# One pool for exponents and front input, the last projection in other banks, the gate copied in pieces, later query loads and reordered out phases

## Chip, cores and metric

The kernel runs on one core of one Trainium2 chip. The metric is the time of one execution in microseconds of the device; lower is better. "PE" is TensorE, "DVE" VectorE, "ACT" ScalarE, "POOL" GpSimd, "SP" the engine that only issues DMAs here.

## What is computed

Two attention branches on one input x (2048 positions of 512 values, float32), mixed by a gate for each position:

```python
g = sigmoid((x * gate_w).sum(-1, keepdims=True))
# A: 32 heads of 16; each position looks at 8 positions, 2 apart, at and before it
qkv = (x @ wqkv).reshape(B, S, 3, H, Dh).transpose(2, 0, 3, 1, 4)
idx = pos[:, None] - 2 * arange(8)[None, :]           # masked where negative
a = (softmax(q . k[idx] * Dh**-0.5) @ v[idx]) @ wo
# B: 32 query heads of 16 on one shared key and value head, no mask
s = einsum("bhqd,bkd->bhqk", x @ wq (by heads), x @ wk) * Dh**-0.5
b = (softmax(s) @ (x @ wv)) @ wo
out = g * a + (1 - g) * b
```

Branch B is the heavy one: 32 heads of 2048 x 2048 scores.

## The kernel before

**Units and steps.** Branch B is cut into NU = 32 units: 512 queries (NQB = 4) times 4 heads (NHG = 8). A unit has 16 block steps, one for each 128 keys, so there are NS = 512 steps. A step multiplies keys and queries into two double banks of PSUM (`eb[0]` and `eb[1]`, named pe in the profile; `exp_pair`, L425), ACT takes the exponent of each (L427) into a tile `pexp`, and `weighted` (L435) multiplies values and exponents into the bank `po`, one step behind. The softmax's maximum is subtracted inside the score product: two extra rows of the query tile hold the maximum of each query, split in two parts. So before a unit's steps its 64 maxima over key blocks must be there. They are found by "filling": a score product into another bank (`m2`, named pm, a double bank; `m1`, named ps; in the front `po` too; L301) and a maximum on DVE, L322 for the double bank (two maxima), L333 for a single one. In the front, `fill_diff` and `fill_sum` find two key blocks' maxima at once from sums and differences of key halves (L375, L384 on ACT, L394 on DVE). `shift_a`, `shift_c` and `shift_b` bring a unit's maxima into its query tile `qst`.

**The front.** Before the blocks there are 78 "lumps" of matmuls in one list, written by `stream`: 14 lumps of queries (two more come earlier) and 64 of branch A's projections (4 groups of heads `gg` times 16 blocks of positions `j`). Lump x goes to `eb[x % 2]`. A product of full precision is made of three products of a shorter format: x is kept as a high part `xh` and a rest `xl`, and the weights likewise. A query lump's result is copied by ACT (`two`, L199), added by POOL (`qraw`), rounded by ACT (`qhi`), its rest taken by POOL (`qlo`, two buffers), and both parts go to DRAM through SP (`queries_out`, L189). Then `stack` (L274, L275) loads them, four DMAs for a unit, into one of NB = 8 tiles `qst`. A projection lump's result is copied by ACT (L238), added by DVE into `stage` (L243; the first group also into the values and the gate, L245 and L246) and stored to DRAM by a DMA on ACT's queue (L250). `half_keys` makes the sums and differences of key halves at lumps ("a", 0, 4) and ("a", 0, 6). `gates` turns the gate's 2048 values into the layout of the blocks, in 16 small copies (L263).

**The blocks.** After the last lump the front's pool is released and the pools of the second phase take its place. For each step the program writes the exponent pairs, fillings between them, and the product of the step before. The order in a step is `(0, "m2", 1, "m1")`; for the first step and after an out phase it is `(1, "m2", 0, "m1")`. POOL computes branch A beside this, group by group.

**Out phases.** Four times, `out_phase` projects 4 blocks of 128 positions with both output weights: `prepare` splits branch B's part (ACT L582, POOL L584), `turn` transposes branch A's part on PE (L591, into `eb[k]`) and splits it (ACT L597 and L598, POOL L605), the matmuls are L689, and `out_store` copies the result (`two`, ACT L624).

**Who sets the order.** The whole order is fixed when the program is built. A small planner keeps a clock for PE, ACT and DVE (`clk`), due times of banks (`free`) and of postponed work (`tasks`), with fixed costs; at every point it writes the work that its clock says is ready. Engines run their own instructions in order and wait on semaphores. What the planner does not charge, it does not see.

## Time and profile before

| what | us |
|---|---|
| median of 3 runs | 1550.73 (1546.35 to 1551.43) |
| the profiled execution, its own time | 1548.13 |
| span of that execution, first to last instruction | 1546.4 |
| PE busy | 1498.4 |
| DVE busy | 1290.7 |
| ACT busy | 1220.0 |
| POOL busy | 934.7 |

The mean granted TensorE clock was 0.992. In the profile's rows "L427" is a line of the kernel; a row of a timeline has the start, the time taken, engine, line, operation, what is written and read, and in brackets the idle time of the engine before it and what ended that; "PEld" is the load of weights, which runs beside matmuls. A row of the waits has the sum in us, the number of waits and the longest. Matmuls overlap in the rows, so the start of one to the start of the next tells its cost.

### The profile page before, as it was taken

To read this page: it belongs to the slowest core of one execution; us is meant where nothing else is said; L and a number is where in the kernel's file an instruction comes from. 1 tells how busy PE (TensorE), PEld (TensorE's weight loads), DVE (VectorE), ACT (ScalarE), POOL (GpSimd) and SP (SyncE) were. 2 spreads that over 40 slices of the span, in tenths; PEclk is the share of its full clock that TensorE was granted. 3 is DMA by queue.
4 is the path that set the end of the run, shared out by engine and by line. 5 is a ranking of instruction groups with operands and counts; after the bars stand their busy time and mean duration, and the time that the engine had idled before them with its cause. 6 is when DMAs were issued, how large, how long until landed. Compare 5 with 4: busy or idle time off the path is not lost.

```text
span 1546.4 us, 29008 instructions
## 1 busy us (share of the span) xinstructions
PE 1498.4 (97%) x11020; PEld 720.5 (47%) x11020; DVE 1290.7 (83%) x1937; ACT 1220.0 (79%) x1490; POOL 934.7 (60%) x1525
## 2 busy tenths in 40 slices
PE   7899999899999999999999999999999999999997
PEld 4788999533333333333333453333345335433532
DVE  6887888789888989989898898998889889887811
ACT  4447776589999989999899749989875985799686
POOL 7731898698898888888889888884022003100310
PEclk9999999899999999999999999999999999999999
DMA  6643243221121122112112112110000000000000
GB/s 213 186 115 120 88 149 92 70 75 47 40 74 57 39 75 74 47 40 74 40 39 72 57 41 72 40 40 11 12 18 23 11 2 15 15 1 1 1 1 28
DMA packets 44019, 85.63 MB, mean 55 GB/s; under 512 B 9616, under 2 KB 26072, under 8 KB 39784
## 3 DMA queue, kind: packets, MB, share of 16 engines
q0 software_dynamic: 6816, 37.97, 7.4%
q1 hardware_dynamic: 19160, 31.40, 6.8%
q10 hardware_dynamic: 17904, 14.42, 2.9%
q8 instruction: 86, 1.41, 0.4%
q14 instruction: 53, 0.43, 0.1%
HBM read 57.97 MB, written 25.25 MB: 54 GB/s over the span
## 4 chain that ended last, share of the span: by engine, by line
PE 87%; ACT 5%; DVE 5%; DMA 1%; POOL 1%; issue 1%; SPq 1%; DVEq 0%; ACTq 0%; POOLq 0%
PE po L435 30%; PE pe L425 21%; PE pm L301 9%; PE pe L894 9%; PE ps L301 8%; PE pe L689 5%; ACT pexp L427 4%; DVE mx L322 2%; PE pm L375 2%; PE ps L375 1%; PE pe L172 1%; PE po L375 1%; DVE mx L333 1%; DMA xraw<-xt 0%; DMA qd<-qlo 0%
## 5 line engine op out<-in xcount | busy, mean ns | idle before, releaser
L427 ACT ACTIVATE pexp<-pe 128x1024 f32<-128x1024 f32 x1022 | 988.8, 1022 | 106.7 <-PE pe L425 100.2
L322 DVE TENSOR_REDUCE mx<-pm 128x2 f32<-128x1024 f32 x565 | 688.2, 1218 | 131.3 <-PE pm L301 126.7
L435 PE MATMUL po<-pexp,vst 128*32 128x512 f32 x4088 | 545.3, 605 | 0.5 <-ACT pexp L427 0.4
L425 PE MATMUL pe<-qst,kst 64*128 64x512 f32 x2048 | 467.1, 453 | 16.4 <-ACT pexp L427 7.6
L425 PEld LDWEIGHTS pe<-qst,kst 64*128 64x128 f32 x2048 | 191.8, 184 | 523.8 <-ACT pexp L427 503.4
L333 DVE TENSOR_REDUCE mx<-ps 128x1 f32<-128x512 f32 x556 | 377.6, 679 | 7.3 <-PE ps L301 6.6
L301 PE MATMUL pm<-kst,qst 62*128 62x512 f32 x1140 | 241.1, 410 | 3.2 <-DVE mx L322 1.9
L301 PE MATMUL ps<-kst,qst 62*128 62x512 f32 x556 | 227.5, 409 | 0.7 <-DVE mx L333 0.7
L495 POOL TENSOR_TENSOR pr<-aext 128x256 f32<-128x256 f32 x256 | 182.1, 737 | 4.7 <-PE pe L894 4.5
L548 POOL TENSOR_TENSOR oa<-oa,av 128x256 f32<-128x256 f32 x224 | 163.9, 732 | 17.3
L435 PEld LDWEIGHTS po<-pexp,vst 128*32 128x32 f32 x4088 | 80.4, 108 | 175.6 <-issue 162.3
L461 POOL TENSOR_TENSOR rl<-rl,gate_t 128x16 f32<-128x16 f32 x31 | 6.8, 219 | 249.7 <-DVE rl L455 249.7
L545 POOL TENSOR_TENSOR av<-aext,lg 128x256 f32<-128x256 f32 x224 | 139.3, 622 | 13.5
L301 PEld LDWEIGHTS pm<-kst,qst 62*128 62x128 f32 x1140 | 111.4, 187 | 28.1 <-DVE mx L322 23.0
L894 PE MATMUL pe<-wah,xh 64*128 64x384 f32 (+1 forms) x512 | 117.7, 349 | 4.8 <-DVE gate L246 3.3
L894 PE MATMUL pe<-wah,xl 64*128 64x384 f32 (+1 forms) x512 | 118.2, 342 | 0.0
L894 PE MATMUL pe<-wal,xh 64*128 64x384 f32 (+1 forms) x512 | 118.0, 342 | 0.0
L384 ACT ACTIVATE dd<-pm 128x512 f32<-128x512 f32 x162 | 88.5, 596 | 35.7 <-PE pm L375 31.8
L301 PEld LDWEIGHTS ps<-kst,qst 62*128 62x128 f32 x556 | 104.1, 187 | 26.6 <-DVE mx L333 21.1
L501 POOL TENSOR_TENSOR tr<-pr 128x512 f32<-128x512 f32 x64 | 81.6, 1276 | 4.9
L501 POOL TENSOR_TENSOR tr<-tr 128x256 f32<-128x256 f32 (+1 forms) x128 | 72.3, 565 | 9.2
L894 PEld LDWEIGHTS pe<-wah,xh 64*128 64x128 f32 x512 | 72.6, 190 | 10.8 <-issue 5.6
(157 smaller groups left out, 1523.3 us busy)
## 6 DMA issues: line engine op xcount, KB each, us to landing
aext<-ad POOLq DMA_DIRECT2D x32, 1056.0 KB, 5.5
ad<-stage ACTq DMA_DIRECT2D x32, 384.0 KB
qst<-qd SPq DMA_DIRECT2D x64, 128.0 KB
xraw<-xt SPq DMA_DIRECT2D x16, 256.0 KB
qd<-qhi SPq DMA_DIRECT2D x16, 256.0 KB
qd<-qlo SPq DMA_DIRECT2D x16, 256.0 KB
qst<-qd SPq DMA_DIRECT2D x64, 64.0 KB
qst<-ml SPq DMA_DIRECT2D x220, 2.0 KB
```

Source lines behind the costliest of these rows:

```text
L301: nc.tensor.matmul(dst, qst[v % NB][b:b + 62, pr, t * P:(t + 1) * P], kst[b:b + 62, kc * 512:(kc + 1) * 512], start=True, stop=True)
L322: nc.vector.tensor_reduce(m[:, :, pr, t, kc], dst, AX.X, ALU.max)
L333: nc.vector.tensor_reduce(m[:, odd, pr, t, kc:kc + 1], dst, AX.X, ALU.max)
L384: nc.scalar.activation(dd[0][:, odd], m2[:, odd, :], AF.Abs)
L425: nc.tensor.matmul(bank[:, odd, :], kst[b:b + 64, kt * P:(kt + 1) * P], qst[u % NB][b:b + 64, pr, :], start=True, stop=True)
L427: nc.scalar.activation(e, bank, AF.Exp, scale=SCALE)
L435: nc.tensor.matmul(po[32 * i:32 * i + 32, :], vst[:, kt, :], pexp[s, i // 2][:, i % 2, :], start=(kt == 0), stop=(kt == NJ - 1))
L495: nc.gpsimd.tensor_mul(pr[:, k], q, e[:, o:o + NH, AC:2 * AC])
L501: nc.gpsimd.tensor_add(nx, cur[:, :, 0:n], cur[:, :, n:2 * n])
L545: nc.gpsimd.tensor_mul(av, e[:, o:o + NH, 2 * AC:].rearrange("p j (h d) -> p j h d", d=DH), lg[:, w].unsqueeze(3).to_broadcast([P, NH, AG, ...
L548: nc.gpsimd.tensor_add(ao, ao, av)
L894: nc.tensor.matmul(eb[x % 2][:, b, :n], l[h], r[h], start=(i == 0), stop=(i == 3 * C - 1))
```

## The change

Seven edits.

1. A pool `px` with six tiles lives through the whole kernel. The first three quarters of `xh` are six tiles of it, the last quarter is in the front's pool, and all exponents (`pexp`, and the last output tiles) take the same six tiles in turn. The tile `early` for the first step is gone.
2. The last lump writes to `m2` instead of `eb[1]`. Its list entry settles the posts of the two lumps before it and issues both exponent pairs of step 0, after its third and its eighth group of matmuls. From the last group but one of the lump before it, `ended` stops the fillings into `m2`; the sums and differences stay selected until the list's end (`formed.clear()` moves there), so no new single filling is written either.
3. After the list, the posts and the store are settled; the wait of 0.7 us on the planner's clock and two fillings are gone.
4. `gates` puts its 16 copies into `tasks`, 3 us apart, and charges 0.24 us for each.
5. `half_keys` writes only the matmuls; copies and sums come as a task 1 us later, both copies first, and the banks count as taken for 4 us.
6. `stack` is no longer called for units 4 to 7 after query lumps 2 and 3, but for one unit after each of the lumps 5, 7, 9 and 11.
7. An out phase's first `prepare` is written one step before the phase, its first `turn` after two groups of matmuls of the phase, and the rest of that split after seven. The step keeps its usual order of banks.

```diff
+    px = ctx.enter_context(tc.tile_pool(name="exps", bufs=6))
-    xh = [p1.tile([P, C, 512], F32R, name="xh", tag=f"xh{t}", bufs=1) for t in range(NQB)]
+    xh = [[px.tile([P, 2, 512], F32R, name="xh", tag="pexp", bufs=6) for k in range(2)] for t in range(3)]
+    xh.append([p1.tile([P, 2, 512], F32R, name=f"xh3{k}") for k in range(2)])
...
-            for u in (2 * m, 2 * m + 1):
-                if u < NB:
-                    stack(u)
+            if m > 4 and m % 2 and len(stacked) < NB:
+                stack(len(stacked))
...
-        for i in range(HG):
-            for b in range(4):
-                nc.scalar.activation(gate_t[32 * i:32 * i + 32, :, :, b], gate[32 * b:32 * b + 32, 1, :].rearrange("p (q j) -> p q j", j=4), AF.Copy)
+        for k in range(16):
+            tasks.append((clk["pe"] + 3.0 * (k + 1), gates_of, (32 * (k // 4), k % 4)))
+
+    def gates_of(i, b):
+        nc.scalar.activation(gate_t[i:i + 32, :, :, b], gate[32 * b:32 * b + 32, 1, :].rearrange("p (q j) -> p q j", j=4), AF.Copy)
+        after("act", 0, 0.24)
...
         clk["pe"] += 1.2
+        for k in keys:
+            free[k] = clk["pe"] + 4.0
+        tasks.append((clk["pe"] + 1.0, half_parts, (g, keys)))
+
+    def half_parts(g, keys):
         for x in range(2):
-            parts, src = kcd[0][:, g, x], hb[g][x]
-            nc.scalar.activation(parts, src, AF.Identity, scale=mk[:, 0:1])
-            at = after("act", clk["pe"] + T_LAT, 0.6)
-            nc.vector.scalar_tensor_tensor(parts, src, mk[:, 1:2], parts.bitcast(F32), op0=ALU.mult, op1=ALU.add)
+            nc.scalar.activation(kcd[0][:, g, x], hb[g][x], AF.Identity, scale=mk[:, 0:1])
+            at = after("act", clk["pe"], 0.65)
+        for x in range(2):
+            parts = kcd[0][:, g, x]
+            nc.vector.scalar_tensor_tensor(parts, hb[g][x], mk[:, 1:2], parts.bitcast(F32), op0=ALU.mult, op1=ALU.add)
...
-        e = e or pe[0].tile([P, 2, 512], F32, name="pexp", bufs=6)
+        e = px.tile([P, 2, 512], F32, name="pexp", bufs=6)
...
-            if paired():
+            if ended:
+                pass
+            elif paired():
...
     def out_phase(js, n):
-        prepare(js[0], n)
-        turn(js[0], 1)
-        later.pop(js[0])()
...
+            if x == 0 and i == 1:
+                turn(j, 1)
+            if x == 0 and i == 6:
+                later.pop(j)()
...
-        nc.tensor.matmul(eb[x % 2][:, b, :n], l[h], r[h], start=(i == 0), stop=(i == 3 * C - 1))
+        nc.tensor.matmul(front[2 if x == last else x % 2][0][:, b, :n], l[h], r[h], start=(i == 0), stop=(i == 3 * C - 1))
...
-        if x == last and i == 4:
-            early.append(p1.tile([P, 2, 2, 512], F32, name="early", tag="xh0", bufs=1))
-            exp_pair(0, 0, early[0][:, 0])
+        if x == last - 1 and i == 3 * C - 2:
+            ended.add(1)
+        if x == last and i in (2, 7):
+            settle(f"post{(i - 1) % 2}", 0)
+            exp_pair(0, int(i == 2))
...
+    front = [(eb[0], "e0"), (eb[1], "e1"), (m2, "m2")]
...
-    clk["pe"] += 0.7
-    settle("post0", 0)
-    settle("post1", 0)
-    fill_ready("m2", 0.5)
-    fill_ready("m1", 0.5)
-    exp_pair(0, 1, early[0][:, 1])
+    formed.clear()
+    for kind in ("post0", "post1", "store"):
+        settle(kind, 0)
...
-            out_phase(list(range(outs, outs + 4)), n)
-            outs += 4
-            order = (1, "m2", 0, "m1")
+            if not due:
+                prepare(outs, n)
+                due.append(n)
+            else:
+                out_phase(list(range(outs, outs + 4)), due.pop())
+                outs += 4
```

The rest of the diff follows from these: `xh[t][:, c, :]` becomes `xh[t][c // 2][:, c % 2, :]`, and due times are looked up by the bank's key.

More of the change, by code (lines that the diff above doesn't have):

```diff
@@ L115, in split_x @@
         for c in range(C):
-            split(xh[t][:, c, :], xl[:, t, c, :], xraw[t, c], eng)
+            split(xh[t][c // 2][:, c % 2, :], xl[:, t, c, :], xraw[t, c], eng)
     def load_wa(gg, c):
@@ L183, in queries @@
         cs = slice(cc * P, (cc + 1) * P)
-        return three(lambda c: wqh[:, c, cs], lambda c: wql[:, c, cs], lambda c: xh[qb][:, c, :], lambda c: xl[:, qb, c, :])
+        return three(lambda c: wqh[:, c, cs], lambda c: wql[:, c, cs], lambda c: xh[qb][c // 2][:, c % 2, :], lambda c: xl[:, qb, c, :])
     def queries_out(m, hi, lo):
@@ L222, in a_project @@
         t, r = j // 4, slice(j % 4 * P, (j % 4 + 1) * P)
-        return three(lambda c: xh[t][:, c, r], lambda c: xl[:, t, c, r], lambda c: wah[gg][:, c, :n], lambda c: wal[gg][:, c, :n])
+        return three(lambda c: xh[t][c // 2][:, c % 2, r], lambda c: xl[:, t, c, r], lambda c: wah[gg][:, c, :n], lambda c: wal[gg][:, c, :n])
     def a_post(gg, j, x):
-        bank, n = eb[x], GN + (0 if gg else VN)
+        (bank, key), n = front[x], GN + (0 if gg else VN)
         settle("post0", 0)
@@ L239, in a_post @@
         at = after("act", clk["pe"] + T_LAT, 0.45) + 0.1
-        free[f"e{x}"] = at + 1.5
+        free[key] = at + 1.5
         def rest():
@@ L246, in rest @@
                 nc.vector.tensor_add(gate[:, 1, j:j + 1], bank[:, 0, GN + DH:GN + DH + 1], two[:, GN + DH:GN + DH + 1])
-            free[f"e{x}"] = after("dve", at, 0.5 if gg else 0.75) + 0.1
+            free[key] = after("dve", at, 0.5 if gg else 0.75) + 0.1
             if j % 2 == 1:
                 dst = ad[gg * GC:(gg + 1) * GC, HALO:, :].rearrange("g (p j) n -> p g (j n)", j=NJ)
-                tasks.append((free[f"e{x}"], lambda: nc.scalar.dma_start(dst[:, :, (j - 1) * AN:(j + 1) * AN], st.rearrange("p g j n -> p g (j n)")), (), "store"))
+                tasks.append((free[key], lambda: nc.scalar.dma_start(dst[:, :, (j - 1) * AN:(j + 1) * AN], st.rearrange("p g j n -> p g (j n)")), (), "store"))
             if j == NJ - 1:
-                tasks.append((free[f"e{x}"] + 0.5, whole, (gg,)))
-        tasks.append((at, rest, (), f"post{x}"))
+                tasks.append((free[key] + 0.5, whole, (gg,)))
+        tasks.append((at, rest, (), f"post{x % 2}"))
     def gates():
@@ L335, in fill_one @@
         filled(v, 1)
-    sel, kcd, dd, pend, ready_d, formed = [], [], [], [], [0.0, 0.0], set()
+    sel, kcd, dd, pend, ready_d, formed, ended = [], [], [], [], [0.0, 0.0], set(), set()
     hb = [(m2[:, 0, :], m2[:, 1, :]), (m1, po)]
@@ L415, in shift_b, with exp_pair @@
         shifted.add(v)
-    pe, pexp, exped, early = [], {}, {}, []
-    def exp_pair(s, pr, e=None):
+    pe, pexp, exped = [], {}, {}
+    def exp_pair(s, pr):
         bank, key = eb[pr], f"e{pr}"
@@ L642, in stream @@
         at, told = [0, 0], 0
+        ended.clear()
         while min(at) < len(seq):
@@ L886, in mm @@
                 half_keys(1 if lump[2] == 4 else 0)
-            elif x == last:
-                formed.clear()
             items[x] = queries(lump[1]) if lump[0] == "q" else a_project(*lump[1:])
-            clk["pe"] = max(clk["pe"], free[f"e{x % 2}"])
+            clk["pe"] = max(clk["pe"], free["m2" if x == last else f"e{x % 2}"])
         n = 512 if lump[0] == "q" else GN + (0 if lump[1] else VN)
@@ L916, in done_mm @@
             gg, j = lump[1:]
-            a_post(gg, j, x % 2)
+            a_post(gg, j, 2 if x == last else x % 2)
             if gg + 1 < C:
@@ L942, in gated_mix_kernel @@
     pe.append(tc.alloc_tile_pool(name="weighted", bufs=1, side="right"))
-    outs = 0
+    outs, due = 0, []
     for s in range(NS + 1):
@@ L960, in gated_mix_kernel @@
         k, n = outs // 4, C - (outs >= NJ - 4)
-        if outs < NJ and outs // NH in done and (NHG * (k + 1) - 1 in shaped if n == C else s >= 16 * (NU - 2) + 4) and (lead < LEAD or s >= 16 * (NHG * (k + 2) + 1) - 3):
-            out_phase(list(range(outs, outs + 4)), n)
-            outs += 4
-            order = (1, "m2", 0, "m1")
+        if due or outs < NJ and outs // NH in done and (NHG * (k + 1) - 1 in shaped if n == C else s >= 16 * (NU - 2) + 4) and (lead < LEAD or s >= 16 * (NHG * (k + 2) + 1) - 3):
+            if not due:
[4 more added lines that the diff above has]
+                outs += 4
         elif short > 0 and steps < 2:
@@ L1010, in gated_mix_kernel @@
             j = NJ - 4 + 2 * x + t
-            os = pe[0].tile([P, D], F32, name="osl", tag="pexp", bufs=6)
+            os = px.tile([P, D], F32, name="osl", tag="pexp", bufs=6)
             nc.vector.tensor_add(os, eb[x][:, t, :], parts[j])
```

## Prediction

> **What bounds the kernel now.** I read the page first, for shares, then PE's own waits, then the clock stretch by stretch, and then the order of events around each long wait.

> ```profile
> PE 1498.4 (97%) x11020; PEld 720.5 (47%) x11020; DVE 1290.7 (83%) x1937; ACT 1220.0 (79%) x1490; POOL 934.7 (60%) x1525
> ```

> PE is the bound: busy 1498.4 of 1546.4 us. An edit that leaves the matmuls alone can win only in the other 48 us, and in stretches where busy matmuls ran at half clock. PE's waits say where the 48 us are:

> ```profile
> PE pe L425 <- ACT pexp L427: 7.6, 20, 2.1
> PE pe L425 <- ACT two L624: 5.0, 4, 1.5
> ...
> PE pe L894 <- ACT two L199: 4.1, 1, 4.1
> PE pe L894 <- DVE gate L246: 3.3, 3, 1.7
> PE pe L425 <- DVE stage L243: 2.6, 2, 1.7
> PE pm L375 <- ACT dd L384: 2.4, 1, 2.4
> PE pe L425 <- ACT early L427: 1.1, 1, 1.1
> PE pe L591 <- ACT pexp L427: 1.7, 4, 0.5
> ...
> PE pe L689 <- POOL own L584: 1.2, 1, 1.2
> ```

> Each row but the first is a place that the diff touches: L199 the query lumps, L246 the half keys, L384 the gate, L243 and "early" the hand-over from front to blocks, L624, L591 and L584 the out phases. The clock (PEclk) by windows:

> ```profile
> 60.00:63.70 3.70, 0.00 (x0) 0.00 (x0) 1.65 (x3) 1.25 (x2) 3.62 (x4) 1.00 0.70 204
> 63.70:67.10 3.40, 3.05 (x14) 2.49 (x16) 0.51 (x1) 1.37 (x3) 3.06 (x4) 0.50 0.60 154
> ...
> 149.00:155.90 6.90, 5.72 (x34) 5.52 (x36) 3.65 (x10) 4.15 (x9) 3.48 (x6) 0.51 0.95 360
> ...
> 282.20:285.60 3.40, 1.70 (x16) 1.36 (x16) 3.37 (x6) 0.35 (x1) 3.24 (x13) 1.00 0.37 116
> 285.60:289.00 3.40, 3.40 (x22) 3.10 (x18) 3.07 (x4) 1.03 (x2) 3.17 (x5) 0.50 0.02 5
> 289.00:292.40 3.40, 1.39 (x10) 0.76 (x9) 1.96 (x3) 1.50 (x2) 1.92 (x5) 1.00 0.25 77
> 292.40:302.70 10.30, 8.19 (x35) 2.88 (x31) 3.96 (x5) 4.62 (x5) 4.66 (x14) 0.50 0.04 14
> ```

> Columns are stretch, length, then busy time of PE, PEld, DVE, ACT, POOL, the clock, DMA. The granted clock halves in the stretch behind a long wait: after the L199 wait, after the L384 wait, and twice at the hand-over. In those stretches half of PE's busy time is loss. So a stall costs its idle time and about half of the busy time behind it.

> **The change part by part**, against the profiled execution's own 1548.13 us (span 1546.4). The median of the runs, 1550.73, is 0.17% above it.

> *Query loads later.* Before, the loads of units 4 to 7 sit on SP between the stores of the query halves:

> ```profile
> 47.09 0.54 SPq L189 DMA_DIRECT2D qd<-qlo  x1
> 49.80 0.58 SPq L274 DMA_DIRECT2D qst<-qd  x1
> ...
> 56.31 0.55 SPq L189 DMA_DIRECT2D qd<-qlo  x1
> ```
> ```profile
> 59.83 1.25 POOL L209 TENSOR_TENSOR qlo<-qraw,qhi 128x512 fp32r<-128x512 f32 x1 [6.12 <-DMA qd<-qlo]
> ```

> The store at 56.31 stood behind eight loads that began at 49.80; POOL waited 6.12 us for its landing to reuse one of two qlo buffers; ACT's qhi and two (L199) wait behind POOL, and PE behind them. After the change the same 16 load issues (4 units of 4, none added) come behind the stores of lumps 5, 7, 9 and 11, and read data stored three or more lumps earlier. One unit's loads hold SP for 4 x 0.58 = 2.3 us, less than a lump, so no store should be late. The gain is 4.1 us idle plus half of 3.05, 5.6 us; DVE, which paces the maxima there, was idle only 2.05 + 2.89 = 4.9 us in these two windows. I take 5.2. The loads' cover: unit 3's maxima end, by ACT's mh instruction, at

> ```profile
> 197.45 0.31 ACT L400 ACTIVATE mh<-mt,mk 128x32 fp32r<-128x32 f32 x1
> ```

> so unit 4's queries are wanted only then, and the query lumps, with the loads among them, are over by 100 us. If a load were late, DVE would run out of maxima.

> *Half keys.* The L246 waits are 3.3 us; the longest, 1.7, follows a chain in which ACT and DVE alternate:

> ```profile
> 108.96 0.75 DVE L366 SCALAR_TENSOR_TENSOR kcd<-pm,mk,kcd 128x512 fp32r<-128x512 f32 x1 [1.53 <-ACT kcd L364]
> 110.47 0.75 DVE L366 SCALAR_TENSOR_TENSOR kcd<-pm,mk,kcd 128x512 fp32r<-128x512 f32 x1 [0.76 <-ACT kcd L364]
> ```

> Both ACT halves first takes out the 0.76; issuing them as a task 1 us later lets DVE pass other work through in the 1.53. Bounds: nothing, and 3.3. I take 1.2. The instructions stay the same.

> *Gate in pieces.*

> ```profile
> 145.20 3.82 ACT L263 ACTIVATE gate_t<-gate 32x16 f32<-32x16 f32 x16 [0.74 <-DVE gate L260]
> ```

> Sixteen copies in a row hold ACT 3.82 us, and the Abs (L384) behind them hold PE 2.4 us. One every 3 us delays an Abs by 0.24 at most. Gate_t is first read in the blocks, 48 us of pieces later and still in the front, so that is covered. Gain 2.4, plus half of 5.72: 5.3, or 2.4 if the clock stays low for another reason. ACT has room (4.15 of 6.90 busy even then).

> *Hand-over.* The last projection goes to the pm banks, both exponent pairs of block step 0 run inside it, and exponents live in one pool with no release ahead of them. Before:

> ```profile
> 293.22 1.93 PE L435 MATMUL po<-early,vst 128*32 128x512 f32 x8
> ...
> 295.27 1.94 ACT L427 ACTIVATE pexp<-pe 128x1024 f32<-128x1024 f32 x2 [3.58 <-PE po L435]
> ```
> ```profile
> 302.94 0.16 PEld L435 LDWEIGHTS po<-pexp,vst 128*32 128x32 f32 x8 [0.47 <-issue]
> ```

> ACT stood still 3.58 us, until step 0's own product ended (293.22 + 1.93). By the code its first exponent tile took memory of the front's released pool, which that product still read; the changed pool has no such neighbour. Idle time here is 1.7 + 0.9 (the two L243 waits), 1.1 (early) and 2.1 (pexp) = 5.8 us; half clock costs half of 3.40 and of 8.19, 5.8 us; together 11.6. New on ACT is the order: exponents of step 0, copy of the last projection, its store (which waits for DVE, with the exponents of step 1 behind it on ACT's queue, and PE's step 2 behind them). I charge 1 us for that (0 to 3.6, the upper end with a new half-clock stretch): gain 10.6. The first six exponent buffers held input whose last matmul is five lumps back or more, so they add no wait.

> *Out phases* (four). Preparation comes a step earlier, transposes go inside the first product, and the next step takes bank 0 first.

> ```profile
> 1180.06 1.02 ACT L624 ACTIVATE two<-pe 128x1024 f32<-128x1024 f32 x1 [6.62 <-PE ps L301]
> ```
> ```profile
> 1182.27 1.07 PE L435 MATMUL po<-pexp,vst 128*32 128x512 f32 x8
> ...
> 1184.80 1.06 PE L435 MATMUL po<-pexp,vst 128*32 128x512 f32 x8
> ```

> At each end PE waits 1.2 to 1.5 us for the bank that ACT is emptying, then takes 2.53 us for the next step. Bank 0 is long free, so its exponents can start first, and the 1.02 us copy is then beside a matmul: 0.6 us from the first, and 0.4 from the second step, since the bank order no longer flips: 4 x 1.0. At the starts the L591 waits, 1.7 us in four, and the L584 wait, 1.2, have work ahead of them now; against that the transposes wait for bank 1, some 0.3 each: 1.7 + 1.2 - 1.2 = 1.7. I take 5.0 in all, after 0.7 for the earlier copy on ACT; the ends are 2.5, if POOL is later than one step and bank 1 late as well, and 6.9.

> *Fewer maxima in the front.* The front runs maxima (L322 two each, L333 one, L394 two) beside its lumps:

> ```profile
> L394 DVE CUSTOM_DVE_ANT_0 dd<-ps,dd 128x512 f32<-128x512 f32 x81 | 55.7, 688 | 25.4 <-PE ps L375 10.5 <-ACT dd L384 7.9 <-ACT mx L295 5.9
> L394 DVE CUSTOM_DVE_ANT_0 dd<-po,dd 128x512 f32<-128x512 f32 x81 | 55.7, 688 | 2.0 <-ACT two L238 0.7 <-PE pe L894 0.3
> L322 DVE TENSOR_REDUCE mx<-pm 128x2 f32<-128x1024 f32 x29 | 35.3, 1216 | 9.0 <-PE pm L301 8.9
> ...
> L333 DVE TENSOR_REDUCE mx<-ps 128x1 f32<-128x512 f32 x29 | 19.7, 678 | 0.3 <-PE ps L301 0.3
> L333 DVE TENSOR_REDUCE mx<-po 128x1 f32<-128x512 f32 x28 | 19.0, 678 | 0.0
> ```

> That is 324 + 58 + 57 = 439 by 291 us. The last lump now runs none (some 11), the half keys hold their banks longer (some 3), the gate's pieces and the hand-over cost a few: about 21 move into the blocks. A block step with three maxima takes 2.13 us, one with two is ACT's:

> ```profile
> 410.06 1.06 PE L435 MATMUL po<-pexp,vst 128*32 128x512 f32 x8
> ...
> 412.19 1.07 PE L435 MATMUL po<-pexp,vst 128*32 128x512 f32 x8
> ```
> ```profile
> 1409.30 1.06 PE L435 MATMUL po<-pexp,vst 128*32 128x512 f32 x8
> ...
> 1413.32 1.06 PE L435 MATMUL po<-pexp,vst 128*32 128x512 f32 x8
> ```

> 2.13 against 4.02 / 2 = 2.01: a maximum that finds such a step costs 0.12. Some 20 late steps, from 1405 to 1446 us, have two. Beyond those a maximum must stand alone, in a pause paced by DVE at 1.216 a pair, 0.61 each. I take 21 x 0.12 = 2.5; the ends are 0 and, with ten alone, 8.

> Sum: 5.2 + 1.2 + 5.3 + 10.6 + 5.0 - 2.5 = 24.8 us; 1548.1 - 24.8 = 1523.3 in a profile, 1526 as a median (0.17% more). Unit steps, tail and first 29 us stay.

> **Rivals.** *The half clock stays.* If the stretches at 149 and behind 282 have another cause than the waits just ahead of them, the 2.9 and 5.8 us of half clock do not come back: 1526 + 8.7 = 1535. [...] Against it stand the rows: 1.70 of 3.40 us idle at 282, 2.01 of 3.40 at 289, and half clock right behind each. I go by the rows.

> *Only half of the hand-over and of the out phases comes.* DVE was 3.37 of 3.40 us busy just before the hand-over, so the last copies may be late for bank 0; then 5.3 + 2.5 us stay: 1534.

> *The stores stand behind the loads again.* If a load waits for the store just ahead of it on SP, four stalls replace one: up to 4 x 5.6 lost where 5.2 was won, 1526 + 28 = 1554 at the worst, and 1526 + 16 = 1542 if two of them show. For it: at 47.09 to 49.80 SP did wait between a store and its load. Against it: those loads read what that store wrote; the new ones don't.

> *Slower: the blocks run out of room for the maxima.* The change saves 27.3 us before this item; the first 20 lost cost 2.4, each further one 0.61, so from about 61 lost of 439 the kernel is slower; at 75 it takes 1526 - 2.5 + 2.4 + 33.6 = 1560. It needs the filling to starve, by later loads or by "ended" stopping it too early. Against it, unit 3 alone lasts until 197 us, and only one lump and part of another are closed.

> **How the numbers follow.** Forecast 0.57 (1518 to 1538 if all its terms were at one end), half clock stays 0.10, half of the hand-over 0.14, stores behind loads 0.09, maxima 0.10. The runs of before spread over 0.33%, so 0.3% (4.7 us) is about what can be told from no change. Faster by more: the first three and a third of the fourth, 0.84; within: 0.05; slower: 0.11. The range 1514 to 1546 leaves out the maxima case, the worst of the stores, and a little below.

> **What would show it.** Right: no PE wait on L199 and no POOL wait on qd; gate_t copies scattered; granted clock 1.00 from 30 us to the tail; the third product of the blocks some 22 us sooner than 302.94; no PE wait on L624 above 0.5. Wrong: any half-clock stretch of over 3.4 us, maxima in the front well under 400, or pairs of maxima late with PE idle between them.

## The result, and the profile after

| | before | after |
|---|---|---|
| median of 5 runs each, us | 1550.73 (1546.15 to 1551.43) | 1538.38 (1536.8 to 1538.94) |
| ratio, 95% interval | | 0.993 (0.9912 to 0.9948) |
| profiled execution, us | 1548.13 | 1536.8 |
| its span, us | 1546.4 | 1535.0 |

Faster by 12.4 us in the medians and by 10.9 by the ratio; 24.7 were forecast. (The runs of before spread with the granted clock: beside the last four experiments they took 1545.25 us at a mean clock of 0.995 and 1553.05 at 0.990.) The time lies inside the range, but half of the gain is missing. The busy times of the page after:

```profile
PE 1494.1 (97%) x11020; PEld 715.8 (47%) x11020; DVE 1291.5 (84%) x1936; ACT 1219.4 (79%) x1488; POOL 939.0 (61%) x1529
```

PE has the same 11020 matmuls and is still the bound. To find the missing half I set the start of each block step's weighted product (L435 before, L445 after) against the same product of the other kernel:

| block step | before, us | after, us | difference |
|---|---|---|---|
| 0 | 293.2 | 276.3 | -16.9 |
| 2 | 302.9 | 282.3 | -20.6 |
| 256 | | | -20.2 |
| 350 | | | -24.4 |
| 454 | 1388.2 | 1359.3 | -28.9 |
| 470 | | | -23.6 |
| 474 | | | -9.3 |
| 511 | | | -11.1 |

(Between steps 256 and 350 lies one out phase, between 350 and 454 two.) Up to step 454 the change had won 28.9 us. It lost 19.6 of them in the twenty steps after and won 1.8 back in the last out phase, so some 18 are missing at the end. PE's own waits of after show what it stood for there; columns are the sum, the number and the longest:

```profile
PE pe L435 <- ACT pexp L437: 5.7, 17, 1.6
...
PE pe L435 <- DVE mx L326: 4.4, 2, 2.6
PE pe L435 <- ACT two L634: 3.1, 4, 0.9
...
PE pe L906 <- DVE stage L244: 2.3, 5, 1.0
...
PE pe L305 <- DVE mx L326: 1.7, 4, 0.6
PE pe L906 <- DVE gate L247: 1.7, 2, 1.2
```

Gone are the long waits on query lumps, on the gate's Abs and on "early". New are two rows in which PE waits for a maximum (L326) to free an exponent bank (pe). Maxima are written into these banks only when the planner finds too few done and puts in a `pause`, in which PE does nothing but fill. DVE's groups of the whole run, by form, name them; before has no such row:

```profile
L326 DVE TENSOR_REDUCE mx<-pe 128x2 f32<-128x1024 f32 x7 | 8.3, 1216 | 0.0
...
L337 DVE TENSOR_REDUCE mx<-pe 128x1 f32<-128x512 f32 x2 | 1.4, 692 | 0.1
```

PE's timeline at the longest pause, in step 471, with 22 maxima (19 by the pause):

```profile
1400.15 1.07 PE L445 MATMUL po<-pexp,vst 128*32 128x512 f32 x8
...
1402.43 0.50 PE L305 MATMUL pe<-kst,qst 62*128 62x512 f32 x2 [0.32 <-DVE mx L337]
1403.56 0.49 PE L305 MATMUL pm<-kst,qst 62*128 62x512 f32 x2 [0.63 <-DVE mx L326]
1404.69 0.72 PE L305 MATMUL pe<-kst,qst 62*128 62x512 f32 x2 [0.64 <-DVE mx L326]
...
1409.21 0.79 PE L305 MATMUL pe<-kst,qst 62*128 62x512 f32 x2 [0.34 <-DVE mx L326]
1412.61 0.79 PE L435 MATMUL pe<-qst,kst 64*128 64x512 f32 x2 [2.60 <-DVE mx L326]
...
1414.61 1.93 PE L445 MATMUL po<-pexp,vst 128*32 128x512 f32 x8
```

From one weighted product to the next it took 1414.61 - 1400.15 = 14.46 us, where a step takes 2.13: pairs of fillings 1.13 us apart, at DVE's pace. By stretches (length; PE, PEld, DVE, ACT, POOL busy; clock; DMA):

```profile
1398.00:1401.40 3.40, 3.40 (x26) 1.18 (x26) 3.08 (x4) 3.20 (x4) 0.00 (x0) 1.00 0.00 0
1401.40:1404.80 3.40, 1.81 (x11) 0.71 (x9) 3.33 (x5) 0.15 (x1) 0.00 (x0) 1.00 0.00 0
1404.80:1418.40 13.60, 9.58 (x35) 3.64 (x39) 10.77 (x13) 2.97 (x4) 0.00 (x0) 0.50 0.00 1
```

ACT, with no exponents to take, is idle, and behind the stretch in which PE is busy for only 1.81 of 3.40 us the granted clock is 0.50 for 13.6 us. Steps 455 to 457 are a smaller case (6 maxima in step 455, 4.3 us lost, half clock for 3.4 us from 1367). With 12.3 and 1.3 at steps 471 and 472 these make up 17.9 of the 19.6; most of the rest went between them, where steps of after still take three maxima and some of before only two.

How many maxima were missing can be counted. Before, up to step 454 (DVE's groups from 0 to 1388.2 us), and after (to 1359.3):

```profile
L322 DVE TENSOR_REDUCE mx<-pm 128x2 f32<-128x1024 f32 x523 | 636.8, 1218 | 116.5 <-PE pm L301 112.2 <-ACT mx L295 1.0
L333 DVE TENSOR_REDUCE mx<-ps 128x1 f32<-128x512 f32 x533 | 361.9, 679 | 6.0 <-PE ps L301 5.2 <-ACT mx L295 0.7
```
```profile
L326 DVE TENSOR_REDUCE mx<-pm 128x2 f32<-128x1024 f32 x515 | 627.2, 1218 | 113.1 <-PE pm L305 108.8 <-ACT mx L299 0.8
L337 DVE TENSOR_REDUCE mx<-ps 128x1 f32<-128x512 f32 x523 | 355.2, 679 | 2.0 <-PE ps L305 1.3 <-ACT mx L299 0.7
```

With the front's sums and single maxima (324, 28 and 10 before; 320, 26 and 10 after) that is 1046 + 533 + 362 = 1941 against 1030 + 523 + 356 = 1909: 32 fewer. Thirteen are lost in the front (428 for 441), nine in three out phases, which are shorter (54, 51 and 55 maxima beside them for 57, 55 and 57), ten in the steps. So the lead of 28.9 us at step 454 was partly borrowed: work that before had done by then was still to do.

### The profile page after: what moved, and what is told of

It reads as the page before. It is cut to its first block, busy times and chain, and to the rows that moved or that the text cites. A ratio compares the mean times of both kernels' runs of the same rounds, so it can differ in the third digit from the quotient of the medians.

```text
span 1535.0 us, 29001 instructions
## 1 busy us (share of the span) xinstructions
PE 1494.1 (97%) x11020; PEld 715.8 (47%) x11020; DVE 1291.5 (84%) x1936; ACT 1219.4 (79%) x1488; POOL 939.0 (61%) x1529
## 4 chain that ended last, share of the span: by engine, by line
PE 87%; DVE 8%; ACT 3%; issue 1%; DMA 1%; SPq 0%; ACTq 0%; DVEq 0%
PE po L445 31%; PE pe L435 22%; PE pm L305 9%; PE ps L305 8%; PE pe L906 7%; PE pe L699 5%; DVE mx L326 4%; ACT pexp L437 2%; DVE mx L337 2%; PE pm L385 2%; PE po L385 1%; PE ps L385 1%; PE pe L174 1%; DMA xraw<-xt 1%; DVE stage L244 0%
## 5 line engine op out<-in xcount | busy, mean ns | idle before, releaser
L326 DVE TENSOR_REDUCE mx<-pm 128x2 f32<-128x1024 f32 x559 | 680.9, 1218 | 127.1 <-PE pm L305 122.5
L445 PE MATMUL po<-pexp,vst 128*32 128x512 f32 x4096 | 547.4, 606 | 1.0 <-DVE tt L459 0.5
L435 PE MATMUL pe<-qst,kst 64*128 64x512 f32 x2048 | 467.2, 453 | 14.1 <-ACT pexp L437 5.7
L435 PEld LDWEIGHTS pe<-qst,kst 64*128 64x128 f32 x2048 | 192.4, 184 | 520.4 <-ACT pexp L437 499.8
L445 PEld LDWEIGHTS po<-pexp,vst 128*32 128x32 f32 x4096 | 80.7, 108 | 177.9 <-issue 165.1
L906 PE MATMUL pe<-wah,xh 64*128 64x384 f32 (+1 forms) x504 | 112.3, 344 | 4.3 <-DVE stage L244 2.3
L394 ACT ACTIVATE dd<-pm 128x512 f32<-128x512 f32 x160 | 87.3, 596 | 35.1 <-PE pm L385 30.8
L906 PE MATMUL pe<-wah,xl 64*128 64x384 f32 (+1 forms) x504 | 112.6, 337 | 0.0
L906 PE MATMUL pe<-wal,xh 64*128 64x384 f32 (+1 forms) x504 | 112.1, 337 | 0.0
L424 POOL DMA_DIRECT2D qst<-ml x40 | 22.8, 574 | 106.1 <-DVE ml L416 105.7
```

What stands on the lines that cost most here:

```text
L326: nc.vector.tensor_reduce(m[:, :, pr, t, kc], dst, AX.X, ALU.max)
L394: nc.scalar.activation(dd[0][:, odd], m2[:, odd, :], AF.Abs)
L435: nc.tensor.matmul(bank[:, odd, :], kst[b:b + 64, kt * P:(kt + 1) * P], qst[u % NB][b:b + 64, pr, :], start=True, stop=True)
L445: nc.tensor.matmul(po[32 * i:32 * i + 32, :], vst[:, kt, :], pexp[s, i // 2][:, i % 2, :], start=(kt == 0), stop=(kt == NJ - 1))
L906: nc.tensor.matmul(front[2 if x == last else x % 2][0][:, b, :n], l[h], r[h], start=(i == 0), stop=(i == 3 * C - 1))
```

## The experiments

My theory: the change runs out of room for the maxima, that is, of places in the steps where a filling fits; the 32 that came to lie behind step 454 cost the 18 us, and the other terms are right. The rival: the terms are only half there, or the late steps are slow for another reason (the new order of banks), whatever the number of maxima. Eight kernels start from `e1_pairs`, the changed kernel with one constant altered. "Before" ran beside every kernel; the ratio is to it.

| kernel | us, median | ratio, 95% interval |
|---|---|---|
| e1_pairs | 1523.77 | 0.9848 (0.9833 to 0.9864) |
| e1_again (the same) | 1524.86 | 0.9847 (0.9832 to 0.9863) |
| e2_fewer | 1519.56 | 0.9821 (0.9805 to 0.9838) |
| e3_more | 1570.26 | 1.0147 (1.0130 to 1.0165) |
| e4_before_pairs | 1548.90 | 1.0009 (0.9996 to 1.0022) |
| e1_m10 | 1525.53 | 0.9842 (0.9827 to 0.9856) |
| f_loads | 1528.94 | 0.9869 (0.9854 to 0.9884) |
| f_gate | 1527.18 | 0.9859 (0.9844 to 0.9874) |
| f_half | 1528.28 | 0.9868 (0.9851 to 0.9885) |
| f_out | 1530.04 | 0.9878 (0.9861 to 0.9894) |
| f_hand | 1526.62 | 0.9846 (0.9832 to 0.9861) |
| f_hand2 | 1528.11 | 0.9864 (0.9846 to 0.9883) |
| a_hand | 1529.72 | 0.9866 (0.9850 to 0.9883) |
| a_hand2 | 1529.03 | 0.9873 (0.9858 to 0.9889) |
| h_only | 1547.29 | 0.9999 (0.9982 to 1.0016) |

### Room for the maxima

**e1_pairs**: a pair of fillings may be written in a step although the plan has its bank free 0.8 us late, where the change allows 0.5.

```diff
-LEAD, M2S, M1S = 1.5, 0.5, 0.3
+LEAD, M2S, M1S = 1.5, 0.8, 0.3
```

> The changed kernel with one constant different: a pair of maxima may be written where its bank comes free up to 0.8 us later than the planner's clock instead of 0.5 (M2S). Theory 'room': the changed kernel loses 18 us between steps 455 and 473 because 32 maxima fewer are done by then than before, so that some 25 have to be done in pauses. With the longer slack the program does 22 more by step 454 and writes no pause: no step of the last hundred above 3 us outside the out phase, no half clock behind 30 us, and 1538 - 18 + 3 (22 waits of some 0.15) = 1523 us. Rival 'early out phases': the stretch at 1400 us comes from out phases two and three lying 23 and 26 steps earlier, which leaves the last units without cover; they lie as early here, so 1538 + 3 = 1541 us.

Measured 1523.77: faster than the change by 15 us in the medians, by 13 in the ratios. 1931 maxima are done by step 454, no pause is written, and where after lost its 18 us PE is never idle:

```profile
1331.00:1400.00 69.00, 69.00 (x482) 24.82 (x480) 61.07 (x74) 62.40 (x66) 3.96 (x8) 1.00 0.01 1
1400.00:1424.00 24.00, 24.00 (x169) 8.04 (x168) 17.96 (x23) 22.62 (x25) 3.11 (x6) 1.00 0.01 2
```

A few more pairs in the steps give back 13 to 15 of the 18 us. They are not free: at step 454 e1_pairs leads before by 22.5 us and not by 28.9. Of these 6.4 us, 1.4 are gone by the third step (half clock at 279 us, see the end); the other 5.0 went by step 454, in which it did 22 maxima more: some 0.23 each, if all of it is theirs. The rival of halved terms falls: with the maxima in place the change wins 24 us over before.

**e4_before_pairs**: the same constant in the kernel before.

> The kernel before with the longer slack of 0.8 us for pairs alone. Theory 'room': there is no pause in it to be saved, so the same time within 2 us: 1549 to 1553 us. Rival: the slack is a gain by itself, as steps that skip a pair are bad for any version: 1540 us or less; then the gain of the first of these runs is not evidence for the pauses.

No gain: the constant is worth nothing where there is no pause. So the 13 to 15 us are not the constant's own.

**e2_fewer**: the change without 32 maxima. Half of unit 5's maxima are left out, so its exponents lack a part of their maximum.

```diff
+    slots = [x for x in slots if not (x[0] == 5 and x[3] >= 2)]
...
-            left[v] = NF // NU
+            left[v] = NF // NU - 32 * (v == 5)
```

> The changed kernel with 32 maxima less: for unit 5 only the first half of the keys is looked at for the maximum (left out on purpose; the softmax only takes another shift). Theory 'room': no pause, 1538 - 18 - 2 = 1518 us, and up to step 454 the same lead of 29 us over the kernel before. Rival 'early out phases': these stay about where they are in the changed kernel, so the stall at steps 455 to 473 stays and 1536 us.

**e3_more**: before, with 32 maxima of unit 20 found twice.

> The kernel before with 32 maxima more: for unit 20 those over the second half of the keys are done twice. Theory 'room': the kernel before had about ten to spare, so this one has to do 25 in pauses as the changed kernel does, and is slower than before by some 18 us: 1550.7 + 18 = 1569 us, with a half-clock stretch around 1410 us. Rival 'early out phases': its phases move by some steps only, so 32 x 0.04 to 0.12 us: 1552 to 1555 us.

Both went as the theory of room said: 17 to 19 us less (ratios, medians) and 23 us more for 32 maxima, 0.5 to 0.7 us each. In e3_more the long waits of after appear in the old order of the steps, between 1390 and 1450 us, with the same lengths:

```profile
PE pe L426 <- DVE mx L323: 4.4, 2, 2.6
PE pe L302 <- DVE mx L323: 2.1, 4, 0.6
```

So they do not need the new order of the banks.

**e1_m10**: 1.0 in place of 0.8.

> e1_pairs with a step further: a pair of maxima may start in a step that is short of it by 1.0 us on the plan, where e1_pairs has 0.8. By the room theory nothing is left to win, since e1_pairs has no pause: 1521 to 1526, the same time. If lateness of pairs costs PE, it is slower by the added waits: 1528 or more. If fillings are still what the late steps lack, faster: below 1520.

1525.53, the same time as e1_pairs within the intervals: with no pause left there is nothing more to win.

### The terms one by one

**f_loads**: e1_pairs with the query loads where they were (edit 6 undone).

> The version with the longer slack for pairs (1523.8 us), with the query loads back behind lumps 2 and 3. The order of matmuls is the same to the last one, so only the stall differs. Theory (the prediction's step): POOL waits for a qlo store behind eight loads, PE 4 us, and 3.4 us run at half clock: + 5.7 us, 1529.5. Rival: POOL's own chain of 3.4 us a lump bounds the query lumps, so the PE stall only moves: + 2 us or less, 1526 us.

The first step of the blocks came 5.4 us later, with the old stall and the old half clock:

```profile
60.10:63.50 3.40, 0.00 (x0) 0.00 (x0) 1.44 (x3) 1.31 (x2) 3.32 (x4) 1.00 0.67 196
63.50:66.90 3.40, 3.11 (x14) 2.47 (x16) 0.57 (x1) 1.37 (x3) 3.07 (x4) 0.50 0.60 154
```

**f_gate**: the 16 copies in a row again (edit 4 undone).

> The same version with the gate's 16 copies in one row again. Theory: PE waits 2.4 us for an Abs and some 6 us run at half clock; + 5.3 us, 1529 us. [...]

The first step came 4.6 us later: one wait of 4.2 us, for a projection's sum (L244) and not for an Abs, and 3.40 us at a clock of 0.50 behind it, so the prediction's clock rival falls. The front did four maxima fewer (424), 1929 were done by step 454, and the planner wrote one in a pause: step 471 took 3.40 us, 1.3 more than usual.

```profile
137.50:140.90 3.40, 0.29 (x4) 0.29 (x6) 0.56 (x1) 3.28 (x13) 0.82 (x2) 1.00 0.62 209
140.90:144.30 3.40, 3.40 (x24) 3.31 (x24) 1.78 (x5) 1.18 (x4) 1.35 (x2) 0.50 0.98 408
```

**f_half**: the half keys inline again (edit 5 undone).

> The same version with the half keys' copies and sums back in line, ACT and DVE in turn, and no hold of 4 us on their banks. Theory: the edit is worth what the first group's lumps showed, 3 us, of which the maxima that it takes cost some: 1525 to 1527 us. Rival 'room': it takes more maxima than it is worth, the planner does ten more by step 454 without it: 1522 us or less.

Larger than I had it: first step 6.6 us later. The stretch of the half keys itself gives 2 to 4 of it (at projections 8 to 20). The rest comes ahead of projection 24, at 157 us, with half clock from 161.5 to 164.9 (0.50); PE's waits between 150 and 166:

```profile
PE ps L379 <- DVE mx L398: 3.0, 1, 3.0
```

It waits 3.0 us for a sum's maximum. Why undoing the half keys brings that later wait I did not separate. The rival's ten maxima did come (1941 by step 454 for 1931), but with no pause to save they won nothing that shows.

**f_out**: the out phases as before (edit 7 undone).

> The same version with out phases as before: preparation, transposes and split ahead of the first product, and bank 1 first afterwards. Theory (the prediction's step): + 5.0 us, 1529 us, with 1.2 us waits on the copy after each phase. The traces of the changed kernel suggest more, some 7: 1531 us. Rival: ACT's extra copy one step earlier and the wait on bank 1 give it back: + 1 us, 1525 us.

The last block step came 4.8 us later. The waits on the output copy, in f_out and in e1_again:

```profile
PE pe L435 <- ACT two L634: 4.7, 4, 1.2
```
```profile
PE pe L435 <- ACT two L634: 3.1, 4, 1.0
```

**h_only**: the hand-over alone (edits 1 to 3) on e4_before_pairs, everything else as before.

> Of the change only the hand-over (edits 1 to 3: shared pool, last projection in the pm banks, both exponent pairs inside it), on the kernel before with a pair of maxima allowed in a step that is 0.8 us short of it, as in e1_pairs and e4_before_pairs (1548.9). The sum's term alone: 1548.9 - 10.6 = 1538, plus some 4 us for six maxima that the plan puts into two pauses at steps 473 and 474: 1538 to 1543. If the term is worth nothing by itself: 1549 to 1553.

The third weighted product starts at 290.69, in e4_before_pairs at 300.73:

```profile
290.69 1.06 PE L440 MATMUL po<-pexp,vst 128*32 128x512 f32 x8
```
```profile
300.73 1.06 PE L435 MATMUL po<-pexp,vst 128*32 128x512 f32 x8
```

10.0 us won, 0.3 to 1.1 of them ahead of the last lump. Yet the whole kernel gained only 1.6 us, less than the intervals tell: 21 maxima fewer in the front (420 for 441), 1925 by step 454, a pause, and half clock for 10.2 us:

```profile
1412.90:1416.30 3.40, 1.82 (x13) 0.67 (x7) 3.33 (x5) 1.80 (x2) 0.00 (x0) 1.00 0.02 5
1416.30:1426.50 10.20, 9.33 (x34) 3.38 (x34) 4.62 (x9) 4.05 (x5) 0.00 (x0) 0.50 0.00 0
```

I had priced this pause at 4 us and missed again on the same term: the gain fell from 10.0 us at step 470 to 1.4 at step 474, so it cost 8.6 (four maxima above three a step), about half of that (half of 9.33) in clock.

**f_hand and a_hand**: the hand-over undone but for the shared pool, on e1_pairs and on the change. In these two the first exponent pair overwrites the bank of the last projection but one before its sum has read it, so that sum adds scores in place of a projection; f_hand2 and a_hand2 settle the sum first and stand for them.

> e1_pairs with the hand-over put back as it was (last projection in eb[1], fillings open in the last lump, first exponent pair after the fifth group, second after the list), but with the shared pool of six tiles kept. The forecast gave 10.6 us to the whole hand-over and the traces 9.8, without saying which half of the edit earns it. If the pool does (the 3.58 us for which ACT stood for memory of the released pool, and the half clock behind it), this costs 2 to 4 us: 1526 to 1528, with waits on the stage sums (L244) near 268 but none of over 1 us on an exponent tile. If the bank and the exponents inside the last lump do, it costs 8 to 10: 1532 to 1534, with half clock of over 6 us at the hand-over. The front's maxima go from 428 to 437 by either, which should be worth nothing here, as there is no pause.

> The changed kernel (1538.4) with the same hand-over put back and the shared pool kept, nothing else altered. The last lump fills again, nine maxima more in the front (437 for 428). Theory: the closed lump took the maxima whose lack costs 18 us at steps 455 to 473; nine more there leave fewer behind later ones, the planner writes no pause, and the kernel is faster though its hand-over is worse: 1538.4 - 18 + 2 to 4 = 1522 to 1525, or 1530 if the bank change is worth 10. Rival: the number of maxima in the front doesn't matter and the long steps come from the order of the blocks' steps: 1540 to 1548, with the same long steps near 1400.

> e1_pairs with the hand-over as before (last projection in eb[1], fillings open in the last lump, exponent pairs after the fifth group and after the list), the shared pool kept, the sums of the bank settled ahead of its exponent pair. If the pool earns the hand-over's gain: 0 to 3 us over e1_pairs of the same call (the trace of f_hand lost 5.3 us at the first block step, of which 3.5 came back by the end). If the bank and the exponents inside the last lump earn it: 8 to 10 us over.

> The changed kernel with the same hand-over, nothing else altered: nine maxima more in the front. Theory of the closed lump: no pause and no long step near 1400, so 1538.4 - 18 + 0 to 5 = 1520 to 1526, up to 1530 with the half clock at the hand-over that a_hand showed. Rival (long steps come from the order of the blocks): 1538 to 1545.

f_hand2 is 2.6 us slower than e1_again by the ratios (the intervals leave -1 to 6): first step 6.1 later, third 3.6, the end 3.0. Between a_hand2 and the change the third step differs by 4.8. So the other bank and the exponents inside the last lump earn some 3 to 5 of the hand-over's 10 us. By subtraction the other 5 to 7 belong to the pool; no run undoes the pool alone. a_hand2, the change with the old last lump, beats the change by 9 us. It does 11 maxima more by the first block step (439 for 428) and 1934 by step 454, and from 1350 to 1500 PE waits for no maximum at all:

```profile
PE pe L435 <- ACT pexp L437: 2.6, 10, 0.3
PE pe L435 <- ACT two L634: 1.0, 1, 1.0
```

Of the kernels that leave nothing out e1_pairs is the fastest, and e1_m10 the same within the intervals: 24 us below before and 13 to 15 below the change.

## Why the prediction was half right

| term | forecast | before to after | in experiments |
|---|---|---|---|
| query loads | 5.2 | 5.5 | 5.4 (f_loads) |
| half keys | 1.2 | 3 | 2 to 6.6 (f_half) |
| gate | 5.3 | 5 | 4.6 (f_gate) |
| hand-over | 10.6 | 9.2 to 10.4 | 9 to 10 (h_only) |
| out phases | 5.0 | 7.1 in four, with 11 maxima fewer | 4.8 (f_out) |
| all but the maxima | 27.3 | 28.9 at step 454, partly borrowed | 24 (e1_pairs, whole run) |
| maxima | -2.5 | -18 | -13 to -15 (e1_pairs), -17 to -19 (e2_fewer) |

The hand-over is read from the starts of the last two lumps to the third block step. An out phase is read from the step before it to the step behind it; 5.2 us of the 7.1 come in the three phases up to step 454. Between projections 20 and 62 (of 0 to 63) after gave 2.7 us of its lead back; its waits on projections' sums (L244) are 2.1 us there, where before has 0.8, and the rest is not separated. The rest of the lead at step 454, some 3 us, came in steps that did fewer maxima.

In the experiments the undone terms are read at the first block step, the out phases at the last. By the third step some 1.5 us of each of the three terms of the front are gone again, since e1_pairs has a half-clock window at 279 us (0.51 up to 282.4 in e1_again; mean clock 0.998 in both) that f_loads, f_gate and f_half do not have (their mean clock of 0.999 leaves at most 4.6 us of half clock, and 3.4 of it stand behind the undone stalls). By the ratios of whole runs the single edits cost 1.7 to 4.7 us, each uncertain by some 3, since a kernel that loses time in the front also fills differently later.

**What was right.** PE is the bound, and the gain lies in waits and in half clock behind them. The clock rival falls: after has no half clock from 30 to 1367 us, and the undone stalls of f_loads, f_gate and f_half each brought some back, 3.4 us at 0.50 (f_half's behind its later wait). The measured time alone would not have told: 1538 is near the 1535 of this rival and the 1534 of the halved terms. The stores are not behind the loads: no L199 wait is left. The order on ACT at the hand-over costs 1.6 us, where 1 was charged:

```profile
277.03 1.94 ACT L437 ACTIVATE pexp<-pe 128x1024 f32<-128x1024 f32 x2 [1.04 <-DVE stage L244]
...
279.02 0.50 PE L435 MATMUL pe<-qst,kst 64*128 64x512 f32 x2 [1.63 <-ACT pexp L437]
...
282.30 1.06 PE L445 MATMUL po<-pexp,vst 128*32 128x512 f32 x8
```

The exponents of step 1 wait 1.04 us behind the store that waits for DVE's sum, and PE's step 2 waits 1.63 behind them. The third product came 20.6 us sooner; "some 22" were said. L634's waits did not fall below 0.5 as said; the longest fell from 1.5 to 0.9.

**The step that failed** is the last term, "21 x 0.12 = 2.5". The number was too small: I counted what the front loses (21 forecast, 13 measured), and not that shorter out phases and faster steps find fewer maxima too, 19 more. And the spare room was wrong: "some 20 late steps, from 1405 to 1446 us, have two" maxima. The planner wants a unit's maxima seven steps ahead of it: unit 29's (30 x 64 = 1920 in all) at step 457, unit 30's (1984) at step 473, and there it wrote the pauses. The steps I counted are 462 to 482, so half of them lie behind the second due time and give no room. The counts by step 454 show the bound: 1909 (after) and 1925 (h_only) lead to pauses, 1931 (e1_pairs), 1934 (a_hand2) and 1941 (before) to none. The small pause of f_gate, at 1929, fits between. Before thus had some 10 to spare, not 20.

The price was also too low. A maximum in a step cost up to 0.23 us in e1_pairs, not 0.12. Beyond the room it was put at 0.61, DVE's pace alone. Spread over all 32, e2_fewer and e3_more give 0.5 to 0.7; but ten of the 32 are within the room, and 18 us over the other 22 are 0.8 each. The 0.61 left out half clock (in the long pause's last product 1.93 us stand where 1.06 are usual; in h_only about half of 8.6) and what a pause costs by itself: f_gate's single maximum took 1.3 us. With its own prices and the right numbers, 32 lost and room for ten, the term would have been 10 x 0.12 + 22 x 0.61 = 14.6.

So the rival that I gave 0.10, "the blocks run out of room", is the mechanism that came. I had it make the kernel slower from 61 lost on, since I set it against the whole gain, and gave it no part in the forecast; it took 18 of 28.9 us at 32.

The trace of before could have told it: a planner that skips pairs in late steps shows the room left at the end, but the bound is a due time, and the number to read is how many maxima are done there.

## To carry to other kernels

Where idle slots of one stage pay for work that a later stage needs by a due time, an edit that shortens the first stage spends those slots: count the work done at the due time, in the trace of before, and set that against what the edit takes away everywhere, not only where it is made. A slack that shows behind the due time is not room. Once such a plan overflows, the price is not the work alone but, here, the clock too: behind windows with PE busy for 1.63 and 1.81 (after) and 1.82 (h_only) of 3.40 us it went to 0.50, for 3.4, 13.6 and 10.2 us. Fillings spread over the steps, at up to 0.23 us each, were cheaper than the same work in a pause.

## What the hardware showed

```profile
275.60:279.00 3.40, 1.77 (x13) 0.50 (x15) 1.43 (x3) 2.20 (x3) 2.25 (x4) 1.00 0.38 120
279.00:282.40 3.40, 3.40 (x15) 1.14 (x15) 1.82 (x2) 1.94 (x2) 3.17 (x5) 0.51 0.00 0
```

In after the grid's edge, at 278.4, cuts it in two, and the clock stays:

```profile
275.00:278.40 3.40, 2.22 (x17) 0.56 (x13) 1.43 (x3) 2.36 (x4) 2.26 (x6) 1.00 0.28 83
278.40:281.80 3.40, 2.77 (x21) 1.38 (x22) 1.82 (x2) 2.56 (x4) 3.24 (x5) 1.00 0.12 37
```

So one stall costs some 1.7 us more (an estimate, half of the 3.40 us at 0.51) or not, by where it falls. Part of a term's half clock can thus be luck of where its stall falls. In after the halved clock also held on: of the four windows of the long pause,

```profile
1404.80:1408.20 3.40, 2.32 (x8) 0.80 (x8) 3.40 (x4) 0.00 (x0) 0.00 (x0) 0.50 0.00 0
1408.20:1411.60 3.40, 1.47 (x4) 0.46 (x4) 3.40 (x4) 0.00 (x0) 0.00 (x0) 0.50 0.02 5
1411.60:1415.00 3.40, 2.39 (x11) 1.35 (x15) 2.08 (x2) 1.50 (x2) 0.00 (x0) 0.50 0.00 0
1415.00:1418.40 3.40, 3.40 (x18) 1.03 (x14) 1.89 (x6) 1.46 (x3) 0.00 (x0) 0.50 0.00 0
```

the first three are busy for 2.32, 1.47 and 2.39 us, and the one behind each is halved too; full speed (0.99 from 1418.4 to 1421.8 us) came back only behind the fourth, busy for all of its 3.40 us.
